# Which engine waits for the last store: the wait moved from the sync engine to the tensor engine

## The chip, the cores and the metric

The kernel runs on one core of one Trainium2 chip. The metric is the device time of one execution in microseconds (us). Times quoted are medians of several executions. The profile is one execution with the hardware profiler on, with its own time beside it.

The engines are named as in the profile: PE is the tensor engine, DVE the vector engine, ACT the scalar engine, POOL the GpSimd engine, SP the sync engine. SP issues all the DMA transfers of this kernel. PSUM is the memory that the matmuls write their results to. A semaphore is a counter by which engines wait for each other and for transfers. A store has landed when the last of its data has been counted on its semaphore.

## The reference, cut to what matters

```python
def reference(A_x, A_k_cache, A_v_cache, A_wq, A_wo, B_x, B_W_gate, B_W_up, B_W_down, gate_w):
    x = A_x                                             # [4, 1, 512], bfloat16
    g = _sigmoid((x * gate_w).sum(-1, keepdims=True))
    a = _A_ref(x, A_k_cache, A_v_cache, A_wq, A_wo)     # attention over the last 4096 cached positions
    b = _B_ref(x, B_W_gate, B_W_up, B_W_down)           # gated feed-forward, 512 -> 1792 -> 512
    return g * a + (1 - g) * b                          # [4, 1, 512]
```

For the change only the end matters: the result is 4 rows of 512 bfloat16 numbers, 4 KB, stored with one DMA.

## The kernel before: the parts that matter

Each engine has its own program, made by one Python function. The functions share a small helper: `op` emits an instruction which increments a semaphore when it is done, and `wait` emits a semaphore instruction that holds the engine's sequencer until a count is reached.

```python
    def wait(self, keys):
        ...
        for ctr, val in need.items():
            if self.seen.get(ctr, 0) < val:
                self.eng.wait_ge(self.plan.sems[ctr], val)
                self.seen[ctr] = val
```

The end of the sync engine's program issues the store when both halves of `osum` have been copied, and then waits for it to land:

```python
    def sync(e):
        ...
        load(("OUT",), "d_out", out.rearrange("b o d -> (b o) d"), osum[:, :], waits=[("OSUM", 1), ("OSUM", 0)])
        E.wait([("OUT",)])
```

The other engines end earlier. PE ends with the last matmul of the output projection, ACT and DVE each with a copy of one half of the result from PSUM to `osum`, POOL with the last of its constants, near the start:

```python
    def tensor(t):
        ...
        for it in order:
            if it[0] in fns:
                fns[it[0]](*it[1:])
    # vector:  v.tensor_copy(osum[:, OW:2 * OW], banks[ACC][OR:OR + 4, 0:OW])
    # scalar:  a.activation(osum[:, 0:OW], banks[ACC][0:4, 0:OW], ACTF.Copy)
```

There is no barrier of the kernel's own at its end. Each engine's program simply stops.

## Time and profile before

| | before |
|---|---|
| median of 3 runs (lowest to highest) | 196.03 us (195.95 to 196.17) |
| profiled run: time, span of the kernel's own instructions | 196.06 us, 194.81 us |
| time less span | 1.25 us |
| store: issued, landed, SP's wait over | 193.54, 194.77, 194.81 us |

Four lines of the page of the kernel before: the span, the busy tenths of the DMA engines in 40 slices, and the chain that ended last.

```profile
span 194.8 us, 1734 instructions
...
DMA  6999999999999999999999999999999999999992
...
## 4 chain that ended last, share of the span: by engine, by line
DMA 54%; DVE 31%; PE 9%; issue 4%; SPq 0%; ACT 0%
```

The DMA engines are at nine tenths or more in all slices but the first and the last: the kernel is bound by the stream of its 81 MB of inputs (mean 416 GB/s). The change touches none of it. Only the last slice, of 4.9 us, can matter.

The timeline of the kernel before, at its end (start and duration in us, engine, line, operation, output and input; in brackets the idle time ahead of it and what ended that):

```profile
start us, us, engine line op out<-in xcount [idle before <-releaser]
...
193.06 0.37 ACT L623 ACTIVATE osum<-bank 4x256 bf16<-4x256 f32 x1 [8.90 <-PE bank L320]
193.09 0.42 DVE L577 CAST osum<-bank 4x256 bf16<-4x256 f32 x1 [5.16 <-PE bank L320]
193.54 0.27 SPq L256 DMA_DIRECT2D out_dram<-osum  x1
```

and the waits of the SP queue (who waited for whom: total us, times, longest):

```profile
engine line waited for: us in total, times, longest us
SPq L256 <- DVE kt L491: 120.5, 8, 16.4
SPq L256 <- PE bank L320: 38.5, 8, 14.1
SPq L70 <- ACT osum L623: 8.7, 1, 8.7
SPq L70 <- DMA out_dram<-osum: 1.0, 1, 1.0
SPq L644 <- PEq L644: 0.7, 1, 0.7
```

The line to look at is `SPq L70 <- DMA out_dram<-osum`: SP waits 1.0 us for the store to land, and this is the last thing that the kernel does. The span ends with this wait, at 194.81 us.

The page stops there, but the trace does not. It also holds a record of every increment of every semaphore, with those that are not the kernel's. Here are the last of them, in ns from the start of the span.

```
kernel before
store's semaphore, increments               193971 194668 194691 194730 194774
SP's wait instruction                       194791 to 194808
semaphore 2, first row of nine              193229 193542 193581 193658 | 194924 194968 195006 195041 195088
resets of the semaphores, first and last    195051 ... 195657
semaphore 2, second row of nine             195881 195916 195954 195997 196021 196119 196157 196191 196238
```

The trace has them in this order: nine increments, then one update of each of 229 other semaphores, the kernel's own among them (the first of these 37 ns ahead of the ninth increment), then nine more. The updates are read here as a reset of the semaphores, and each row of nine as a barrier of the five engines. The increments of the second row stand 24 to 98 ns apart, mostly 34 to 47. The author's reading of the nine is a row of engines that is run through to its end and back: each engine makes its increment (a hop) after the one ahead of it, the last in the row makes one and each of the other four makes two, nine in all. Whether that holds, and in which order, is what the experiments below have to show.

The store's own semaphore has one early increment and four late ones. The store has four packets of 1 KB, the first of them starts at 194.279 us, so the increment at 193.971 us stands for no data, and the last of the other four, at 194.774, is taken as the landing.

Read the first row with the ends of the engines in mind. Four increments came early. The fifth came 116 ns after SP's wait was over, and four more followed at once, so the barrier seems to have been standing at its middle, waiting for SP.

### The profile page before, as it was taken

How to read it: one execution, taken by the hardware profiler on the slowest of the kernel's cores; microseconds unless marked ns; L12 is line 12 of the kernel's file. 1: busy time of each engine (PE TensorE's matmuls, PEld its weight loads, DVE VectorE, ACT ScalarE, POOL GpSimd, SP SyncE). 2: the span in 40 equal slices, each digit the busy share in tenths (PEclk: the TensorE clock that was granted, in tenths of full speed). 3: DMA queues.
4: the chain of work that ended last, by engine and by line, in shares of the span. 5: the costliest groups of instructions: out<-in, count | busy, mean ns of one | idle time of the engine just before them, and what ended most of it. 6: DMA issues, size and time to landing. Idle time of an engine off the chain costs nothing.

```text
span 194.8 us, 1734 instructions
## 1 busy us (share of the span) xinstructions
PE 120.6 (62%) x723; PEld 50.6 (26%) x723; DVE 124.1 (64%) x153; ACT 27.5 (14%) x34; POOL 9.5 (5%) x25
## 2 busy tenths in 40 slices
PE   0209279474943894686468943894586466743974
PEld 0003123121411341242112411341142122311562
DVE  6103769999399809980998199819981998370010
ACT  2213000040130013001300130013001300420100
POOL 7830000000000000000000000000000000000000
PEclk9999958999999797899876999697999889997899
DMA  6999999999999999999999999999999999999992
GB/s 215 431 432 431 437 437 431 431 427 451 431 437 437 446 427 424 431 437 431 431 431 431 427 424 437 444 437 431 431 431 421 431 395 427 470 431 384 425 404 90
DMA packets 3616, 81.10 MB, mean 416 GB/s; under 512 B 401, under 2 KB 666, under 8 KB 794
## 3 DMA queue, kind: packets, MB, share of 16 engines
q1 hardware_dynamic: 3610, 81.01, 97.3%
q8 instruction: 5, 0.08, 0.2%
q14 instruction: 1, 0.01, 0.0%
HBM read 81.01 MB, written 0.00 MB: 416 GB/s over the span
## 4 chain that ended last, share of the span: by engine, by line
DMA 54%; DVE 31%; PE 9%; issue 4%; SPq 0%; ACT 0%
DMA slots<-in_A_k_cache_dram 38%; DVE kt L491 21%; DMA slots<-in_A_wo_dram 10%; PE bank L320 7%; DMA xsb<-in_A_x_dram 6%; DVE sc L527 5%; DVE qblk L517 1%; PE bank L324 1%; DVE pT L542 1%; DVE rd L531 1%; SPq L256 0%; DVE negmax L537 0%; ACT gwB L600 0%; DVE osum L577 0%; DVE mx L527 0%
## 5 line engine op out<-in xcount | busy, mean ns | idle before, releaser
L491 DVE STREAM_TRANSPOSE kt<-slots 128x2048 f32<-128x2048 f32 x32 | 73.7, 2305 | 28.1 <-DMA slots<-in_A_k_cache_dram 28.0
L320 PE MATMUL bank<-kt,qblk 128*128 128x512 bf16 x256 | 72.1, 434 | 27.9 <-DVE kt L491 27.9
L320 PEld LDWEIGHTS bank<-kt,qblk 128*128 128x128 bf16 x256 | 25.2, 107 | 69.7 <-DVE kt L491 36.0
L320 PE MATMUL bank<-slots,pT 128*64 128x512 bf16 x256 | 32.3, 410 | 5.7 <-DMA slots<-in_A_v_cache_dram 5.7
L619 ACT ACTIVATE pe<-sc,negmax 128x2048 bf16<-128x2048 bf16 x8 | 16.0, 2002 | 60.1 <-DVE negmax L537 60.1
L527 DVE CUSTOM_DVE_ANT_0 sc<-bank,maskf 128x512 bf16<-128x512 f32 x32 | 21.0, 658 | 3.8 <-PE bank L320 3.7
L320 PEld LDWEIGHTS bank<-slots,pT 128*64 128x64 bf16 x256 | 15.1, 118 | 23.2 <-issue 13.4
L542 DVE STREAM_TRANSPOSE pT<-pe 128x2048 bf16<-128x2048 bf16 x8 | 18.5, 2312 | 2.2 <-ACT pe L619 2.2
L604 ACT ACTIVATE osb<-bank 128x512 bf16<-128x512 f32 x8 | 4.8, 597 | 81.5 <-PE bank L320 81.5
L320 PE MATMUL bank<-rd,grpb 128*128 128x32 bf16 x8 | 1.6, 194 | 22.1 <-DVE rd L531 22.1
L555 DVE TENSOR_TENSOR oq<-bank,recip 64x128 bf16<-64x128 f32 x2 | 0.9, 434 | 12.3 <-PE bank L320 12.2
L320 PEld LDWEIGHTS bank<-rd,grpb 128*128 128x128 bf16 x8 | 0.8, 98 | 25.7 <-DVE rd L531 25.7
L495 DVE COPY xT<-bank 128x20 bf16<-128x20 bf16 x1 | 0.2, 171 | 8.0 <-PE bank L324 8.0
L320 PE MATMUL bank<-slots,oq 128*4 128x256 bf16 x64 | 4.0, 272 | 2.0 <-DMA slots<-in_A_wo_dram 2.0
L320 PE MATMUL bank<-slots,xT 128*4 128x512 bf16 (+1 forms) x64 | 5.0, 467 | 0.0
L320 PE MATMUL bank<-maskr,maskl 128*128 128x512 bf16 x1 | 0.6, 609 | 5.9 <-POOL maskr L296 5.9
L517 DVE TENSOR_SCALAR qblk<-bank 32x64 uint32<-32x64 uint32 x16 | 2.9, 215 | 2.1 <-PE bank L324 2.1
L324 PE MATMUL bank<-identb,xsb 5*128 5x5 bf16 x4 | 0.3, 168 | 5.7 <-DMA xsb<-in_A_x_dram 5.7
L577 DVE CAST osum<-bank 4x256 bf16<-4x256 f32 x1 | 0.4, 418 | 5.2 <-PE bank L320 5.2
L320 PEld LDWEIGHTS bank<-slots,oq 128*4 128x4 bf16 x64 | 2.5, 84 | 3.5 <-DMA slots<-in_A_wo_dram 2.9
L296 POOL TENSOR_SCALAR_AFFINE_SELECT fold<-fold 128x256 bf16<-128x256 bf16 x8 | 3.3, 417 | 1.1
L486 DVE MEMSET qblk<- 128x2304 uint32 x1 | 2.0, 1978 | 1.3 <-PEq L644 1.3
(59 smaller groups left out, 40.3 us busy)
## 6 DMA issues: line engine op xcount, KB each, us to landing
slots<-in_A_k_cache_dram SPq DMA_DIRECT2D x8, 4096.0 KB, 25.1
slots<-in_A_v_cache_dram SPq DMA_DIRECT2D x8, 4096.0 KB, 30.5
slots<-in_A_wq_dram SPq DMA_DIRECT2D x1, 4096.0 KB, 12.4
slots<-in_A_wo_dram SPq DMA_DIRECT2D x1, 2176.0 KB, 17.1
slots<-in_B_W_gate_dram SPq DMA_DIRECT2D x1, 1792.0 KB, 19.7
slots<-in_B_W_up_dram SPq DMA_DIRECT2D x1, 1792.0 KB, 23.6
slots<-in_B_W_down_dram SPq DMA_DIRECT2D x1, 1792.0 KB, 18.5
slots<-in_A_wo_dram SPq DMA_DIRECT2D x1, 1152.0 KB, 19.5
```

Of the source, the lines that this page charges most:

```text
L296: op(lambda: e.affine_select(dst, src, pattern, cmp, fill, base=base, channel_multiplier=mult), ev)
L320: E.op(lambda: t.matmul(out_, lhsT, rhs, start=start, stop=stop, tile_position=pos, skip_group_check=True), ev=ev, waits=waits)
L324: E.op(lambda: t.transpose(out_, in_, idn), ev=ev, waits=waits)
L486: E.op(lambda: v.memset(qblk[:, :, :, :, :].rearrange("p s h c e -> p (s h c e)"), 0.0), ev=("QZ",))
L491: E.op(lambda: v.transpose(kt[:, f, :].bitcast(FP32), slot("k", s)[:, 4096 * f:4096 * f + 4096].bitcast(FP32)), ev=("E", "KT", s, f), waits=w)
L517: E.op(lambda dst=dst, r=r, g=g: v.tensor_scalar(dst, src[r, g, 0:B, :, :], 0, None, op0=ALU.bitwise_or), ev=("E",) + keys[1] if (q, g) == ...
L527: E.op(lambda: v.tensor_tensor_reduce(sc[:, 512 * f:512 * f + 512], banks[scb(key)], R["maskf"][:, :], 1.0, -3.0e38, ALU.add, ALU.max, mx4 ...
L531: E.op(lambda: v.tensor_tensor(rd32[:, :, :], bc(R["own8"][:, :].unsqueeze(2), 2, 4), bc(mx4[:, :].unsqueeze(1), 1, 8), ALU.mult), ev=("MA ...
L542: E.op(lambda: v.transpose(pT[:, s % 2, :], pe[:, :]), ev=("E", "PT", s), waits=[("EXP", s)] + ([("PV", s - 2)] if s >= 2 else []))
L555: E.op(lambda g=g, r=r: v.tensor_tensor(oq[r, :, :].rearrange("p i b -> p b i"), banks[tr(key)][0:64, 128 * g:128 * g + 128].rearrange("p ...
L604: E.op(lambda: a.activation(osb[:, s, :], ob(s), ACTF.Copy), ev=("NORM", s), waits=[("PV", s)])
L619: E.op(lambda: a.activation(pe[:, :], sc[:, :], ACTF.Exp, bias=negmax[:, s % 2:s % 2 + 1], scale=SCALE, accum_out=rowsum[:, s:s + 1]), ev= ...
```

## The change

Its intent is to let SP end as soon as it has issued the store, and have PE, which has nothing left to do either, wait for the landing.

```diff
@@ sync
         load(("OUT",), "d_out", out.rearrange("b o d -> (b o) d"), osum[:, :], waits=[("OSUM", 1), ("OSUM", 0)])
-        E.wait([("OUT",)])
@@ tensor
         for it in order:
             if it[0] in fns:
                 fns[it[0]](*it[1:])
+        E.wait([("OUT",)])
```

## The prediction

> **What bounds the kernel now.** The chain of waits is DMA 54%, DVE 31%, PE 9%; the slices show the DMA engines 90% busy or more from the second slice to the last but one (mean 416 GB/s). None of that is touched: the change moves one semaphore wait at the very end, after the last transfer is issued. Only the tail counts.
>
> **The tail (timeline, waits of the sync queue).** The last matmul ends at 193.03 us, ACT and DVE copy the halves of osum (0.37 and 0.42 us, to 193.51), SP issues the 4 KB store at 193.54 (0.27 us) and waits 1.0 us for it; its wait instruction ends at 194.81, the end of the span. The store's last semaphore increment stands at 194.77 in the trace's semaphore records. PE, ACT, DVE and POOL have been done since 193.0, 193.4, 193.5 and 12 us.
>
> **What the change removes, adds, moves.** No matmul, copy or DMA changes; the order on DVE, ACT and SP is identical, PE gets one wait after its last matmul. The landing is still the last event; the wait for it runs on PE instead of SP. Two differences remain.
>
> 1. Waking. A PE semaphore instruction takes 51 ns in this trace against 17 ns on SP, and starts 28 ns after the landing it waits for (W_down load) against 17 ns. So the last instruction ends 0.045 us later: span about 194.85.
>
> 2. The barrier after the program. The semaphore records show increments of one semaphore that is not the kernel's at 193.23, 193.54, 193.58, 193.66, then, 0.116 us after SP's wait ends, 194.92, 194.97, 195.01, 195.04, 195.09, and only then are all semaphores reset (195.05 to 195.66). [...]the records agree with 35 to 47 ns a hop. By arrival times I read the order as PE, ACT, POOL, DVE, SP and back (an inference from when PE, ACT and DVE end). SP is then the turning point, the best place for a late arriver: 4 hops follow. PE is the worst: all 8 follow. Extra: 4 hops of about 0.04, 0.16 us. PE may also arrive more slowly: 0.21 us stand between its last (modelled) matmul end and the increment, against 0.116 for SP, so 0 to 0.1 us more.
>
> Estimated sum: 0.045 + 0.16 + 0.05 = +0.25 us, all on the critical path. The timed figure exceeds the span by 196.06 − 194.81 = 1.25 us in the profiled run, so I take the timed window to include barrier and resets; if not, only the 0.045 us are seen.
>
> **Prediction.** 196.25 us, 8 in 10 between 195.95 and 196.55. Faster by over 2%: 0.005, within 2%: 0.99, slower: 0.005.
>
> **What would show each step.** Timeline unchanged to the store's issue (193.5 ± 0.3); the wait for out_dram gone from SP's waits and standing on PE, 1 us or more; span +0.03 to +0.1. In the semaphore records, no barrier increment before the landing, then nine about 40 ns apart; resets 0.2 to 0.3 us later after the landing than before.
>
> **What would make it wrong.** Another order of engines in the barrier (the shift is then nearer zero or negative); a timed window that ends before the barrier; variation between runs (0.2 us in three), as large as the effect; PE waking more slowly than one semaphore instruction shows.

## The result, and the profile after

| | before | after |
|---|---|---|
| median (lowest to highest), 4 runs each | 196.06 us (195.95 to 196.17) | 196.45 us (196.33 to 196.61) |
| ratio, with its 95% interval | | 1.0021 (1.0003 to 1.0038) |
| profiled run: time, span | 196.06, 194.81 us | 196.44, 194.94 us |
| time less span | 1.25 us | 1.50 us |
| store issued, landed | 193.54, 194.77 us | 193.62, 194.86 us |

A ratio here is the mean time of one kernel's runs over that of the other's of the same rounds, so it is not quite the ratio of the medians quoted beside it. The kernel after is slower by 0.2%. The interval does not hold 1.

The same lines of the page after:

```profile
span 194.9 us, 1734 instructions
...
DMA  6999999999999999999999999999999989999992
...
## 4 chain that ended last, share of the span: by engine, by line
DMA 54%; DVE 29%; PE 11%; issue 5%; SPq 1%; ACT 0%
```

Nothing has moved in the stream. The timeline at the end:

```profile
start us, us, engine line op out<-in xcount [idle before <-releaser]
...
193.14 0.37 ACT L623 ACTIVATE osum<-bank 4x256 bf16<-4x256 f32 x1 [8.61 <-PE bank L319]
193.17 0.42 DVE L577 CAST osum<-bank 4x256 bf16<-4x256 f32 x1 [4.87 <-PE bank L319]
193.62 0.27 SPq L256 DMA_DIRECT2D out_dram<-osum  x1
```

is the same as before but 0.08 us later, and that comes from ahead of the change: the store is *issued* 0.08 us later (193.62 for 193.54). The waits of the SP queue:

```profile
engine line waited for: us in total, times, longest us
SPq L256 <- DVE kt L491: 125.0, 8, 16.5
SPq L256 <- PE bank L319: 20.1, 7, 7.3
SPq L256 <- PE bank L323: 15.1, 1, 15.1
SPq L70 <- ACT osum L623: 8.9, 1, 8.9
SPq L644 <- PEq L644: 0.7, 1, 0.7
```

The line `SPq L70 <- DMA out_dram<-osum` is gone, as it should be. It does not turn up among PE's waits either; that view names no wait for `out_dram` on PE, presumably since no work follows it there. It is found only among the instructions: PE's semaphore instruction runs from 194.889 to 194.940 us and ends the span.

The semaphore records, in the same form:

```
kernel after
store's semaphore, increments               194052 194749 194779 194811 194861
PE's wait instruction                       194889 to 194940
semaphore 2, first row of nine              195132 195166 195204 195249 195272 195369 195408 195444 195490
resets of the semaphores, first and last    195397 ... 196049
semaphore 2, second row of nine             196274 196308 196346 196390 196414 196512 196550 196584 196631
```

Now no increment stands ahead of the landing. The whole barrier waits for PE, and all nine steps follow PE's arrival. From the landing to the ninth increment it takes 629 ns, where before it took 195088 − 194774 = 314 ns. From there to the end the two kernels are alike: 1150 ns from the ninth increment to the last of the second row before, 1141 ns after.

The time that is measured does include this. In the two profiled runs the measured time lies 0.178 and 0.191 us below the last increment of the second row (196.06 against 196.238, 196.44 against 196.631). In all the eleven profiles, in which that last increment ranges from 196.24 to 197.01 us, the difference is 0.176 to 0.191 us. So the clock is stopped by the end of this closing and not by the end of the kernel.

### The profile page after: what moved, and what is told of

It is laid out like the page before. It is cut to its first block, busy times and chain, and to the rows that moved or that the text cites. A ratio compares the mean times of both kernels' runs of the same rounds, so it can differ in the third digit from the quotient of the medians.

```text
span 194.9 us, 1734 instructions
## 1 busy us (share of the span) xinstructions
PE 121.6 (62%) x723; PEld 51.1 (26%) x723; DVE 124.1 (64%) x153; ACT 27.5 (14%) x34; POOL 9.5 (5%) x25
## 4 chain that ended last, share of the span: by engine, by line
DMA 54%; DVE 29%; PE 11%; issue 5%; SPq 1%; ACT 0%
DMA slots<-in_A_k_cache_dram 38%; DVE kt L491 20%; DMA slots<-in_A_wo_dram 10%; PE bank L319 9%; DMA xsb<-in_gate_w_dram 6%; DVE sc L527 5%; DVE qblk L517 1%; PE bank L323 1%; DVE pT L542 1%; SPq L256 1%; DVE rd L531 1%; DVE negmax L537 0%; ACT gwB L600 0%; DVE osum L577 0%; DVE mx L527 0%
## 5 line engine op out<-in xcount | busy, mean ns | idle before, releaser
L319 PE MATMUL bank<-kt,qblk 128*128 128x512 bf16 x256 | 74.5, 446 | 23.2 <-DVE kt L491 23.0
L319 PEld LDWEIGHTS bank<-kt,qblk 128*128 128x128 bf16 x256 | 26.1, 110 | 67.6 <-DVE kt L491 31.2
L319 PE MATMUL bank<-slots,pT 128*64 128x512 bf16 x256 | 30.8, 396 | 5.1 <-DMA slots<-in_A_v_cache_dram 5.1
```

The source lines that it names most:

```text
L319: E.op(lambda: t.matmul(out_, lhsT, rhs, start=start, stop=stop, tile_position=pos, skip_group_check=True), ev=ev, waits=waits)
```

## The experiments

**Theory A** (the prediction's): what the wait costs is decided by the engine's place in the closing barrier (how many steps follow its arrival) and by the time that the engine itself needs from the landing to its increment. **Rival B**: PE alone is slow; the place in the barrier is of no account. **Rival C**: the difference is only variation of the load stream ahead of the store. **Rival D**: what costs is that SP ends early, whoever waits in its stead.

Every variant is the kernel before with the line `E.wait([("OUT",)])` at the end of another engine's program in place of SP's, or, in `w_sp_pe` and `w_all`, at the end of others besides SP's; `pool_awake` and `pool_work` put something more ahead of it on POOL. All of them gave correct results.

### w_pe: the change again

The diff is that of the change.

> The change itself again, in the same rounds as the next three. Theory A (place in the closing barrier plus the engine's own wake and arrival): from the last landing of the store to the barrier's ninth increment 0.63 us against 0.31 us with SP waiting, so about +0.3 us over before. Rival B (PE is simply slow to wake and arrive, its place does not matter): here also +0.3. Rival C (only variation of the load stream before the store): landing to ninth increment the same as before, and the time difference not repeated. Rival D (what costs is that SP ends early): +0.3 as well; the next three tell.

196.45 us (5 runs) against 196.09 us for before (9 runs); ratio 1.0014 (1.0001 to 1.0026). From the landing to the ninth increment 629 ns, the same as in the first profile of it to the nanosecond, although the store was issued 11 ns later. Rival C cannot explain a closing that repeats so well and that differs from before by 0.315 us.

### w_act: ACT waits

```diff
@@ scalar, after the loop
         for it in act:
             fns[it[0]](*it[1:])
+        E.wait([("OUT",)])
```

> ACT alone waits for the landing. Theory A: ACT is second in the barrier; landing to ninth increment about 0.034 + 0.113 + 0.323 = 0.47 us, +0.16 us over before, about half of PE's. PE's increment stands at about 193.2, before the landing; seven come after ACT's. Rival B: +0.00 to +0.05. Rival C: no difference beyond noise. Rival D: +0.3, as with PE.

196.27 us (5 runs), ratio to the shared runs of before 1.0006 (0.9992 to 1.0019), so the timing alone does not tell it from before. The records do:

```
w_act   landing 194861, ACT's wait over 194899
semaphore 2   193312 | 195012 195051 195095 195118 195216 195254 195290 195337
```

One increment stands ahead of the landing; eight follow it, the first of them ACT's. Landing to ninth increment: 476 ns, which Theory A had put at 0.47. Rival B (0.31 to 0.36) and Rival D (0.63) both fail. ACT wakes and arrives as quickly as SP (38 and 113 ns against 34 and 116), so of the 162 ns over before, 161 are its place in the row.

### w_dve: DVE waits

```diff
@@ vector, after the loop
         for it in dve:
             fns[it[0]](*it[1:])
+        E.wait([("OUT",)])
```

> DVE alone waits. Theory A: DVE is fourth; landing to ninth increment about 0.038 + 0.116 + 0.240 = 0.39 us, +0.08 us over before; the increments of PE, ACT and POOL stand before the landing, and the step from SP's to DVE's second is about 0.10 us, not 0.04, because DVE has only just made its first. Rival B: +0.00 to +0.05. Rival D: +0.3.

196.30 us (5 runs), ratio 1.0009 (0.9996 to 1.0022).

```
w_dve   landing 194925, DVE's wait over 194974
semaphore 2   193377 193691 193729 | 195120 195143 195241 195279 195315 195361
```

Three increments ahead of the landing, as expected of the fourth in the row. Landing to ninth: 436 ns, for which 0.39 was expected; DVE needed 146 ns from the end of its wait to its increment and not 116, and 49 ns to wake and not 38. The step from the fifth to the sixth increment is 98 ns, where it is 44 ns with SP waiting. This was expected: the fourth and the sixth increment are both DVE's, and 121 ns stand between them here. In every closing row where DVE makes its first increment just ahead of SP's, 120 to 123 ns stand between DVE's two. When SP comes late, DVE has long been waiting for it, and answers within 44 ns.

### w_pool: POOL waits

```diff
@@ gpsimd, after the last constant
             aff(v, v, [[1, 4], [-1, 64]], -64 * g, ne, 1.0, ("FOLD", g), mult=4)
+        E.wait([("OUT",)])
```

> POOL alone waits. Theory A: POOL is third; landing to ninth increment about 0.034 + 0.113 + 0.285 = 0.43 us, +0.12 us over before; PE's and ACT's increments stand before the landing. Rival B: +0.00 to +0.05. Rival D: +0.3.

196.59 us (5 runs), ratio 1.003 (1.0017 to 1.0042): slower than before, and by the medians of the same rounds slower than with PE. This is a miss.

```
w_pool   landing 194867, POOL's wait over 194908
semaphore 2   193327 193641 | 195445 195488 195512 195609 195647 195683 195730
```

POOL's place is as expected: two increments ahead of the landing, and 285 ns from POOL's increment to the ninth, exactly the expected figure. What was wrong is the arrival. POOL needs 537 ns from the end of its wait to its increment, where SP and ACT need 116 and 113. In the kernel before this could not be seen, for POOL ends at 12 us.

The five places are now settled by who stands ahead of the landing: none with PE, one with ACT, two with POOL, three with DVE, four with SP. The row is PE, ACT, POOL, DVE, SP, and back.

### w_sp_pe: SP and PE both wait

```diff
@@ both lines
         load(("OUT",), "d_out", ...)
         E.wait([("OUT",)])
@@ tensor, after the loop
+        E.wait([("OUT",)])
```

> Both SP (as before) and PE (as after) wait for the landing. Theory A: the later path decides, so exactly PE alone: landing to ninth increment 0.63 us, +0.3 us over before. Rival D (SP's early end is what costs): SP ends late again, so the time of before, 0.31 us and +0.0.

196.53 us (4 runs) against 196.19 us (7 runs), ratio 1.0016 (0.9999 to 1.0032). SP waits to the end again, as in before:

```profile
engine line waited for: us in total, times, longest us
...
SPq L70 <- ACT osum L624: 8.9, 1, 8.9
SPq L70 <- DMA out_dram<-osum: 1.0, 1, 1.0
```

and yet landing to ninth increment is 628 ns, that of PE alone. So it is not SP's early end that costs, and Rival D falls. SP was through at 195.001 us, PE made the first increment at 195.239.

### w_all: all five wait

The line is put at the end of all five programs.

> All five engines wait for the landing. Theory A: arrivals overlap and do not add; POOL, last to arrive (0.58 us after the landing in the run with POOL alone), decides: landing to ninth increment about 0.86 us, about +0.55 us over before, as with POOL alone. If the waits added up, it would be over 1.2 us.

196.63 us (4 runs) against 196.19, ratio 1.0023 (1.0008 to 1.0038). Landing to ninth increment 864 ns, that of POOL alone (863).

```
w_all   landing 194858
semaphore 2   195129 195163 | 195437 195480 195503 195601 195639 195675 195722
```

The waits overlap. PE's and ACT's increments are made while POOL is still on its way.

### pool_awake and pool_work: why is POOL late?

Two explanations could be told apart: POOL needs half a microsecond at the end of its program whatever it did before (P1), or it was slow because it had been idle since 12 us (P2, put to waits, and P3, put to work). In `pool_awake` POOL has waits to pass shortly before the end; in `pool_work` it does a piece of work there.

```diff
@@ gpsimd, pool_awake
+        E.wait([("E", "OQ")])
+        E.wait([("OSUM", 1)])
+        E.wait([("OUT",)])
@@ gpsimd, pool_work
+        E.op(lambda: e.memset(ones[:, :], 1.0), ev=("LATE",), waits=list(last) + [("OSUM", 1)])
+        E.wait([("OUT",)])
```

> POOL waits in turn for the last oq copy (189 us), the last osum copy (193.6 us) and the landing, so its sequencer has been busy with waits just before. What is open: POOL needed 0.54 us from its wait's end to its barrier increment where SP and ACT need 0.11. Theory P1 (a fixed cost of POOL's ending): 0.54 again. Theory P2 (its sequencer was cold after 183 us of idleness): 0.11 to 0.2, and then about +0.12 us over before instead of +0.5.

> POOL does a memset of 128x128 (values unused) just after the last osum copy, then waits for the landing[...]. P1: 0.54 us from the wait's end to the increment again. P3[...]: 0.11 to 0.2. The result must stay correct.

196.84 us (ratio 1.0033, 1.0018 to 1.0048) and 196.75 us (1.003, 1.0015 to 1.0045), 4 runs each, against 196.19. POOL needed 533 ns from the end of its wait to its increment in both. That POOL did work late in `pool_work` is shown by the timeline of POOL in its last microseconds:

```profile
193.59 0.20 POOL L314 MEMSET ones<- 128x128 f32 x1 [181.52 <-DVE osum L578]
```

The memset ended 0.9 us ahead of the landing at 194.73 us, and nothing came of it. So POOL's long idleness since 12 us is not the reason. The half microsecond passes between the end of POOL's last wait and its increment; what takes that long is not shown by the trace and stays open.

### w_sp: the kernel before once more

> The kernel before, profiled once more on this chip, to see whether the closing sequence repeats where the load stream varies. Theory A: landing to SP's increment 0.15 us and to the ninth 0.31 us again (within 0.03), whatever the time of the store's issue; time as before. Rival C (the closing sequence itself varies by tenths between runs): anything else.

196.14 us (2 runs), ratio 0.9997. In its trace SP's wait instruction, from 194.969 to 194.986 us, is the last of the kernel, as before. The store was issued at 193.713 us, 0.18 us later than in the first profile of the same kernel; landing to ninth increment was 315 ns (314), landing to the end of the second row 1464 ns in both. The stream ahead of the store varies by tenths of a microsecond, the closing, in these two pairs of repeats, by one or two nanoseconds.

### What was not run

A kernel in which nobody waits for the store would bound what the wait is worth. It does not pass the check that a program has to pass before it may go to the chip, which simulates the program and looks for races. It was not run, and what it would save stays open. No experiment pointed to a place better than SP's, so no version beats the kernel before.

### All of them side by side

The parts of the closing, in ns, from the semaphore records of one profile each (for the kernels with several waiters, the one that decides). "Wake" is from the landing to the end of the wait instruction, "arrive" from there to the engine's increment, "row" from there to the ninth, "rest" from the ninth to the end of the second row.

| run | waits | wake | arrive | row | landing to ninth | rest | whole closing | against before |
|---|---|---|---|---|---|---|---|---|
| before | SP | 34 | 116 | 164 | 314 | 1150 | 1464 | |
| w_sp | SP | 34 | 116 | 165 | 315 | 1149 | 1464 | 0 |
| w_dve | DVE | 49 | 146 | 241 | 436 | 1147 | 1583 | +119 |
| w_act | ACT | 38 | 113 | 325 | 476 | 1145 | 1621 | +157 |
| after | PE | 79 | 192 | 358 | 629 | 1141 | 1770 | +306 |
| w_pe | PE | 79 | 191 | 359 | 629 | 1143 | 1772 | +308 |
| w_sp_pe | SP and PE | 79 | 191 | 358 | 628 | 1144 | 1772 | +308 |
| w_pool | POOL | 41 | 537 | 285 | 863 | 1147 | 2010 | +546 |
| w_all | all (POOL decides) | 41 | 538 | 285 | 864 | 1145 | 2009 | +545 |
| pool_awake | POOL | 66 | 533 | 286 | 885 | 1149 | 2034 | +570 |
| pool_work | POOL | 40 | 533 | 286 | 859 | 1148 | 2007 | +543 |

The column "row" is the place in the barrier, and falls from PE (358 or 359) over ACT and POOL to DVE and SP (164) as the row runs. The columns "wake" and "arrive" are the engine's own. Rival B is half right: PE is slower by itself than SP by 45 + 76 = 121 ns, but that is less than half of the 315.

The measured ratios agree within their intervals: 1.0014 of 196.1 us is +0.27 us for w_pe (closing +0.31), 1.0006 is +0.12 for w_act (+0.16), 1.0009 is +0.18 for w_dve (+0.12), 1.003 is +0.59 for w_pool (+0.55).

## Why the prediction was right, point by point

- **The stream is untouched, only the tail counts.** Right. The slices of the DMA engines are at nine tenths in both, but for one at eight. The shares of the chain (DMA 54% in both, DVE 31% and 29%, PE 9% and 11%) say no more: in the second profile of the kernel before they are 47%, 25% and 20%.
- **The time.** 196.25 us was predicted, 196.45 measured, inside the range of 195.95 to 196.55. The range also holds 196.03, the time before, so the hit alone says little; what bears the prediction out is the terms of its sum, below. It was predicted as +0.25 us; the medians of the four runs differ by 0.39. Of the 0.38 us between the two profiled runs, 0.306 are the closing, 0.087 are a later landing that the change does not cause, and the rest is the 0.013 by which the distance between the measured time and the last increment differs.
- **Waking, +0.045 us.** Right: 79 − 34 = 45 ns.
- **PE arrives 0 to 0.1 us more slowly, taken as 0.05.** Right in the range: 192 − 116 = 76 ns.
- **Four more hops of 0.04, 0.16 us.** The mechanism was right and the term too small: 358 − 164 = 194 ns. The four forward steps took 34, 38, 45 and 23 ns, in sum 140. Nearly all of the missing 54 ns is in the turn: DVE's answer to SP took 97 ns after the change and 44 ns before, because before it DVE had been waiting, and after it DVE had made its own first increment only just before. This could have been read ahead of the change: the second row of the kernel before, in which no engine was late, took 196238 − 195881 = 357 ns and had the steps of 24 and 98 in it; less the 164 from SP's increment on, that is 193 ns where the prediction put 160 at 40 a hop.
- **The order PE, ACT, POOL, DVE, SP, taken from arrival times.** Right, and now shown by four kernels with the late arrival put at four other places. That the row is run to its end and back was the author's reading ahead of the runs; the increments that follow the landing bear it out: nine with PE waiting, eight with ACT, seven with POOL, six with DVE, five with SP.
- **The timed window includes the closing.** Right: the measured time follows the last increment of the second row within 15 ns over eleven profiles.
- **What would show it.** No increment ahead of the landing, and resets 0.2 to 0.3 us later after the landing: they begin 0.277 us after it before, 0.536 us after (195397 − 194861), so +0.26. (The prediction has the resets begin only after the ninth increment; they begin 37 ns ahead of it before, and 93 ns ahead after.) "About 40 ns apart" was not right for two of the eight steps (23 and 97 ns). The span grew by 0.13 us and not by 0.03 to 0.1, as the store itself was issued 0.08 us later. And the waits view did not show the wait on PE at all.

Where the expectations failed was POOL: 0.43 us from landing to ninth was expected, by lending it ACT's 113 ns of arrival, and 0.86 was measured.

## What to carry to other kernels

Let the last landing be awaited by an engine that comes late in the closing barrier and is quick to arrive there: here SP is both, and any other choice costs 0.12 (DVE) to 0.55 us (POOL). The place alone is not enough: POOL comes after ACT in the row and costs 0.39 us more. A second waiter does not help and does not add (628 ns from the landing to the ninth increment with SP and PE, 629 with PE; 864 with all five, 863 with POOL): the one whose wake, arrival and remaining row are longest in sum decides. All of this was measured on one kernel, and the parts of ACT and DVE on one profile each. When a change shows in the measured time and not in the span, look at what follows the last instruction of the kernel, in the records of the semaphores that are not yours.

## Further figures of the closing and of the store

- The closing barrier: with four engines already there, it took 0.31 us from the landing to the ninth increment before, and 0.63 us after, when all of it had to follow PE; from the first increment of the row to the ninth it was 1.86 us before, most of it the wait for the store, and 0.36 us after. The cost of a late arrival depends on its place: 164 ns are left after SP's increment, 358 ns after PE's.
- The steps: the last nine increments ahead of the kernel took 371 ns in the trace of the kernel before, and those of the closing row 358 ns from PE's increment to the ninth, after the change. Leaving out the steps held up by a late engine, six of those in the closing rows are 34 to 49 ns, SP's is 23 to 24, and DVE's answer to it is 97 to 99, or 44 when SP is late.
- From the end of an engine's final wait to its increment in the barrier it was 113 ns on ACT, 116 on SP, 146 on DVE, 191 on PE and 533 to 538 on POOL, whether or not POOL had just worked.
- The reset of the semaphores: from its first record to the last, 0.61 us before (195051 to 195657) and 0.65 us after.
- The store: in the eleven profiles its first packet starts 0.74 to 0.75 us after the start of the issuing instruction and 0.47 to 0.48 us after its end. It has landed 1.23 to 1.24 us after the start of the issue.
